# Block-sparse attention and a gated FFN on one core: later attention outputs turned by DMA, a bank of its own for the values, the block mask's spreading matrix made on chip, filler matmuls early, the last FFN groups interleaved

## The chip, the core and the metric

The kernel runs on one core of a Trainium2 chip. Its time is the device time in microseconds (us) of one execution; lower is better. A core has five engines with queues of their own, each of which works its instructions off in order: TensorE (PE in the profile, with PEld for its weight loads), VectorE (DVE), ScalarE (ACT), GpSimd (POOL) and SyncE (SP), which here only issues DMAs. Matmuls write to PSUM, which the kernel divides into eight banks of 2 KB per partition.

## The reference

Attention over 4 batches, 8 heads, 768 tokens and 64 channels, with a mask in blocks of 32 tokens: a block pair is kept when the blocks are neighbours, when one of them is the first or the last, or when it was drawn at random. What attention gives goes, as 3072 rows of 512, through a gated FFN.

```python
scores = scale * np.matmul(q, k.transpose(0, 1, 3, 2))
mask = np.abs(blk_i - blk_j) <= window
mask = mask | (blk_i == 0) | (blk_j == 0) | (blk_i == n_blocks - 1) | (blk_j == n_blocks - 1)
for qb in range(n_blocks):
    for kb in sampled_blocks[qb]:
        mask[qb * block:(qb + 1) * block, kb * block:(kb + 1) * block] = True
scores = np.where(mask, scores, -1000000000.0)
scores = scores - np.max(scores, axis=-1, keepdims=True)
attn = np.exp(scores)
attn = attn / (np.sum(attn, axis=-1, keepdims=True) + 1e-09)
out = np.matmul(attn, v)
x = np.ascontiguousarray(out.transpose(0, 2, 1, 3)).reshape(B * S, H * D)
gate = 1.0 / (1.0 + np.exp(-(x @ w_gate)))
return (gate * (x @ w_val) @ w_out).astype(np.float32)
```

## The kernel before

The work is cut into 12 pieces n (batch b = n // 3, a third c = n % 3 of the queries, 256 of them), and each piece into 4 pairs of heads p. For each pair:

- **scores**: three groups tt of four matmuls (L444) write transposed scores to `st`, a buffer of two banks of which there are two. They use 64 rows of the PE array, two heads side by side ("row" mode).
- **exp** on ACT (L454) from `st` to `pt`, then the multiplication with the 0/1 mask on DVE (L462).
- **values**: 24 matmuls (L476) into `o`, one bank. A column of ones beside the values gives the sums, so that DVE's reciprocal (L484) and multiplication (L487) leave the attention output `x16` with tokens on partitions.
- **turn**: two PE transposes (L500) by the identity turn `x16` into `tT`, which sits in the same bank `o`, and ACT copies it (L505) to `xT`, where channels are on partitions. So each pair goes through the one bank `o` twice.

The **FFN** takes the pieces in the groups [0], [1,2], ... [9,10], [11], that is 256 or 512 tokens at a time. For each of 12 slices f of the hidden width, PE makes gate and value (L525, four matmuls each) in the two banks `gv`; ACT takes the tanh (L540), DVE makes `h` (L545). For each 128 tokens, 12 matmuls (L556) sum the output in `py`, one bank; DVE halves it (L568) into `y`, and SP stores it (L572).

At the **start**, SP loads k, q and v of batch 0 as float32 (L280), 12 transfers of 384 KB. ACT, DVE and POOL cast them to float16 (L305, L295); PE turns k and q by transposes into `gv` (L317), and ACT or DVE copies them out (L321). The mask comes from a 24x24 table of blocks (DVE, L385 to L391), which is spread to tokens with the help of `e24`, a 24x768 matrix of zeros and ones loaded from DRAM by ACT's queue (L261): a product into a buffer `st` (L397, L398), a copy (L401), and then two matmuls for each mask tile (L411) and a copy (L421). The FFN weights follow by POOL's DMA queue (L362, L371). k and q of batches 1 to 3 are cast on POOL and turned by DMA transposes from SP (L329).

**What sets the order.** The kernel records each step as an operation with an engine, a duration, its buffers and a priority; `Plan.run` plays them through on a clock of its own and emits the instructions of each engine in the order that comes out. Smaller priorities go first: attention has 0 to 143, the FFN 10000 and more, so the FFN fills PE where attention isn't ready. Each engine works in order, so an instruction that waits holds up all that stands behind it on that engine.

Of the kernel before, what the change touches and what calls it, by code (L numbers as in the profile page):

```python
# [16 lines left out]
BLK = 32  # L17
# [3 lines left out]
NCH = 3  # L21
# [5 lines left out]
VW = 66  # L27
GROUPS = [[0], [1, 2], [3, 4], [5, 6], [7, 8], [9, 10], [11]]
# [27 lines left out]
class Plan:  # L56
# [3 lines left out]
    def __init__(self):  # L60
        self.ops, self.rings, self.queued = [], {}, {}

# [25 lines left out]
    def run(self):  # L88
# [23 lines left out]
        while left:  # L112
            wake = []
            for e in LAT:
# [4 lines left out]
                for o in todo[e]:  # L119
# [28 lines left out]
                    break  # L148
                if best is None:
                    continue  # L150
# [11 lines left out]
                if o.dma:  # L162
                    dma_free = max(dma_free, now + 1.5) + o.dma
                    o.seen = dma_free + 0.5
                else:
                    o.seen = o.end + o.lat
# [26 lines left out]
def kernel(  # L193
# [14 lines left out]
    tok = NJ * np.arange(128)[None, :] + np.arange(NJ)[:, None]  # L208
    e24_np = (tok.reshape(1, -1) // BLK == np.arange(NB)[:, None]).astype(np.float16)
    e24_h = nc.inline_tensor(e24_np, name="bb_e24")  # L210
# [17 lines left out]
    for name, n in (  # L228
# [3 lines left out]
    ):  # L232
        P.ring(name, n, name != "gv")
# [13 lines left out]
    def one(shape, dt, name):  # L247
# [5 lines left out]
        ident16 = one([128, 128], f16, "ident16")  # L253
# [3 lines left out]
    e24 = one([NB, S], f16, "e24")  # L257
    P.op("ACT", 0.5, lambda: nc.scalar.dma_start(ident16(), id_h.ap()), writes=[ident16], prio=-90, dma=0.3)
    P.op("ACT", 0.5, lambda: nc.scalar.dma_start(sbi(), sampled_blocks), writes=[sbi], prio=-89, dma=0.1)
    P.op("ACT", 0.5, lambda: nc.scalar.dma_start(mi(), mi_h.ap()), writes=[mi], prio=-88, dma=0.1)  # L260
    P.op("ACT", 0.5, lambda: nc.scalar.dma_start(e24(), e24_h.ap()), writes=[e24], prio=-87, dma=0.1)  # L261

    vring = [one([128, 2, NJ, VW], f16, f"v16_{i}") for i in range(8)]
    for i in range(8):
        P.op(
            "POOL", 0.1,
            lambda i=i: nc.gpsimd.memset(vring[i]()[:, :, :, 64:VW], 1.0),
            writes=[vring[i]], prio=-80 + i,
        )

# [4 lines left out]
    def load(nm, b, p, prio, after=(), sync=None):  # L275
# [12 lines left out]
        loads[nm, b, p] = P.op("SP", 0.5, go, writes=[t], prio=prio, after=after, dma=1.22)  # L288

    def cast_v(b, p, prio):  # L290
# [3 lines left out]
            "POOL", 1.0,  # L294
# [4 lines left out]
    def cast_qk(nm, b, p, prio, eng):  # L299
# [3 lines left out]
        P.op(  # L303
            eng, {"ACT": 0.83, "DVE": 0.56, "POOL": 0.95}[eng],
# [4 lines left out]
    def turn_pe(nm, b, p, prio, eng, out_eng):  # L309
        cast_qk(nm, b, p, prio, eng)  # L310
# [8 lines left out]
        P.op("PE", 0.6, go, reads=[c, ident16], writes=[g], prio=prio, mode="full")  # L319
        f = nc.scalar.copy if out_eng == "ACT" else nc.vector.tensor_copy  # L320
        P.op(out_eng, 0.8 if out_eng == "ACT" else 0.55, lambda: f(t(), g()), reads=[g], writes=[t], prio=prio)  # L321

# [14 lines left out]
    for i, (nm, p) in enumerate(order0):  # L337
        if nm == "v":
            last_v = cast_v(0, p, -40 + i)
            if p == 2:  # L340
                gate_w = last_v
        else:
            turn_pe(
                nm, 0, p, -40 + i,
                {"k": "ACT", "q": "DVE"}[nm] if p == 0 else "POOL",
                "ACT" if p == 0 and nm == "k" else "DVE",
# [11 lines left out]
    for a, z in zip(edges, edges[1:]):  # L358
        for nm, t, s in (("g", wg, wgv), ("v", wv, wvv)):
# [4 lines left out]
            o = P.op("POOL", 0.8, go, after=[gate_w], prio=-20 + n, dma=(z - a) * 3.3 / 512)  # L364
# [3 lines left out]
    for s in range(3):  # L368
# [3 lines left out]
            after=[gate_w], prio=-20 + n, dma=3.3,  # L372
# [6 lines left out]
    sbf = one([NB, 3], f32, "sbf")  # L379
    eqs = [one([NB, NB], f32, f"eq{n}") for n in range(3)]  # L380
    mb16, mb24 = one([NB, NB], f16, "mb16"), one([NB, S], f16, "mb24")
    mask = one([128, NCH, NCH, 512], f16, "mask")

    def blocks():
        nc.vector.tensor_copy(sbf(), sbi().bitcast(u16)[:, 0:12:4])  # L385
        for n in range(3):
            nc.vector.tensor_scalar(
                eqs[n](), in0=mi()[:, NB:], scalar1=sbf()[:, n : n + 1], scalar2=None, op0=ALU.is_equal
            )
            nc.vector.tensor_tensor(mi()[:, 0:NB], mi()[:, 0:NB], eqs[n](), op=ALU.max)  # L390
# [236 lines left out]
```

## Time and profile before

| | us |
|---|---|
| median of 8 runs (320.4 to 324.08) | 321.14 |
| the profiled execution, its own time | 320.89 |
| its span (first to last instruction) | 319.1 |
| PE busy, 2852 matmuls | 299.2 |
| DVE busy, 374 instructions | 203.4 |
| ACT busy, 279 instructions | 195.8 |
| POOL busy, 69 instructions | 51.8 |

The span is 1.8 us shorter than the execution's own time. Busy time of PE is modelled with the ends of pipelined matmuls, so a busy PE isn't one at its peak. The rows that follow in the prediction are of this one execution: the chain of work that ended last (start, length, what), windows (busy time in a stretch, number of instructions, granted clock, DMA share, GB/s), groups of instructions (count, busy us, mean ns, idle before and what ended it) and the timeline (start, length, engine, line, operation, xcount, idle before it).

### The profile page before, as it was taken

What the parts mean: (1) busy time and instruction counts of PE and PEld (TensorE: products, weight loads), DVE (VectorE), ACT (ScalarE), POOL (GpSimd) and SP (SyncE); (2) the same over time, 40 slices, a digit from 0 to 9 for tenths busy, and PEclk for the clock granted to TensorE, in tenths of its full rate; (3) what the DMA queues carried; (4) which work ended last, traced back from release to release, by engine and by line L of the source; (5) the groups of instructions that cost most, each with busy time, mean ns of one, the idle gap of its engine ahead of it and who ended that gap; (6) DMA issues with size and microseconds to landing.
All of it is one profiled execution on the core that took longest, in us unless ns stands there. A gap on an engine that the chain in (4) does not pass through costs nothing.

```text
span 319.1 us, 6860 instructions
## 1 busy us (share of the span) xinstructions
PE 299.2 (94%) x2852; PEld 160.7 (50%) x2852; DVE 203.4 (64%) x374; ACT 195.8 (61%) x279; POOL 51.8 (16%) x69
## 2 busy tenths in 40 slices
PE   1998889999999999999999999999999999999994
PEld 1464556644455454545455553455554454445661
DVE  2789988457787877767786687466776343333331
ACT  3569996566788856787995788565686321221120
POOL 1892016453451441000000000000000000000000
PEclk9999999999999999999999999999999999999999
DMA  7999999999995674000001100001000010001101
GB/s 232 335 136 205 205 299 294 295 280 272 326 286 184 92 182 125 33 2 3 0 35 42 59 2 1 2 33 68 35 2 0 1 68 33 35 0 66 69 0 66
DMA packets 41804, 35.12 MB, mean 110 GB/s; under 512 B 20757, under 2 KB 38701, under 8 KB 41773
## 3 DMA queue, kind: packets, MB, share of 16 engines
q1 hardware_dynamic: 35712, 29.89, 33.2%
q0 software_dynamic: 5808, 4.72, 9.6%
q8 instruction: 22, 0.36, 0.5%
q10 hardware_dynamic: 252, 0.08, 0.1%
q14 instruction: 10, 0.07, 0.1%
HBM read 28.39 MB, written 6.29 MB: 109 GB/s over the span
## 4 chain that ended last, share of the span: by engine, by line
PE 68%; ACT 6%; DVE 4%; issue 1%; DVEq 0%; ACTq 0%
PE gv L525 32%; PE py L556 19%; PE o L476 8%; PE st L444 7%; ACT pt L454 5%; PE o L500 1%; DVE h L545 1%; DVE pt L462 1%; ACT tg L540 1%; DVE y L568 1%; DVE x L487 0%; ACT x L505 0%; DVE rz L484 0%; DVEq L545 0%; ACTq L540 0%
## 5 line engine op out<-in xcount | busy, mean ns | idle before, releaser
L454 ACT ACTIVATE pt<-st 128x1024 f16<-128x1024 f32 x144 | 142.9, 1042 | 42.8 <-PE st L444 42.2
L462 DVE TENSOR_TENSOR pt<-pt,mask 128x1024 f16<-128x1024 f16 x144 | 104.9, 738 | 33.6 <-ACT pt L454 33.1
L540 ACT ACTIVATE tg<-gv 128x512 f32<-128x512 f32 (+1 forms) x84 | 46.2, 550 | 59.6 <-PE gv L525 56.0
L525 PE MATMUL gv<-x,wv 128*128 128x512 f16 (+1 forms) x336 | 76.1, 349 | 2.2 <-DVE h L545 1.3
L525 PE MATMUL gv<-x,wg 128*128 128x512 f16 (+1 forms) x336 | 76.2, 349 | 0.8 <-ACT tg L540 0.6
L545 DVE SCALAR_TENSOR_TENSOR h<-tg,gv 128x512 f16<-128x512 f32 (+1 forms) x84 | 51.0, 608 | 38.2 <-PE gv L525 35.6
L556 PE MATMUL py<-wo,h 128*128 128x512 f16 x288 | 70.4, 379 | 0.8 <-DVE y L568 0.8
L444 PE MATMUL st<-qT,kT 64*128 64x256 f16 x576 | 51.3, 281 | 4.7 <-ACT pt L454 4.0
L476 PEld LDWEIGHTS <-pt 128*128 128x128 f16 x1152 | 41.7, 98 | 10.6 <-issue 4.6
L525 PEld LDWEIGHTS <-wv 128*128 128x128 f16 x336 | 30.3, 97 | 32.4 <-issue 10.4
L476 PE MATMUL o<-v,pt 128*128 128x65 f16 x1152 | 45.2, 194 | 0.0
L525 PEld LDWEIGHTS <-wg 128*128 128x128 f16 x336 | 30.3, 98 | 27.0 <-issue 5.2
L556 PEld LDWEIGHTS <-h 128*128 128x128 f16 x288 | 26.1, 98 | 28.4 <-issue 3.4
L444 PEld LDWEIGHTS <-kT 64*128 64x128 f16 x576 | 21.7, 95 | 33.3 <-issue 29.3
L568 DVE TENSOR_SCALAR y<-py 128x512 f32<-128x512 f32 x24 | 16.5, 690 | 19.9 <-PE py L556 19.9
L505 ACT COPY x<-o 128x256 f16<-128x256 f16 x48 | 18.7, 390 | 8.5 <-PE o L500 8.5
L487 DVE TENSOR_TENSOR x<-o,rz 128x256 f16<-128x256 f32 x48 | 20.4, 425 | 1.7
L305 POOL CAST k<-ks 128x768 f16<-128x768 f32 x15 | 14.2, 947 | 43.5 <-DMA ks<-in_k_dram 26.0
L295 POOL CAST v<-vs 128x768 f16<-128x768 f32 x16 | 15.3, 953 | 17.3 <-DMA vs<-in_v_dram 10.1
L305 POOL CAST q<-qs 128x768 f16<-128x768 f32 x15 | 14.0, 936 | 11.3 <-DMA qT<-q 7.7
L484 DVE RECIPROCAL rz<-o 128x4 f32<-128x4 f32 x48 | 8.6, 179 | 11.0 <-PE o L476 10.6
L500 PE MATMUL o<-ident,x 128*128 128x128 f16 x96 | 13.5, 222 | 0.5 <-DVE x L487 0.5
(31 smaller groups left out, 51.1 us busy)
## 6 DMA issues: line engine op xcount, KB each, us to landing
ks<-in_k_dram SPq DMA_DIRECT2D x16, 384.0 KB, 6.2
qs<-in_q_dram SPq DMA_DIRECT2D x16, 384.0 KB, 6.0
vs<-in_v_dram SPq DMA_DIRECT2D x16, 384.0 KB, 5.2
out_dram<-y SPq DMA_DIRECT2D x24, 256.0 KB, 2.0
wo<-in_moe_w_out_dram POOLq DMA_DIRECT2D x3, 512.0 KB, 19.0
wg<-in_moe_w_gate_dram POOLq DMA_DIRECT2D x2, 512.0 KB, 9.7
wv<-in_moe_w_val_dram POOLq DMA_DIRECT2D x2, 512.0 KB, 12.0
wg<-in_moe_w_gate_dram POOLq DMA_DIRECT2D x2, 256.0 KB, 5.4
```

The costliest lines, as they stand in the source:

```text
L305: lambda: f(c(), s().rearrange("p h j d -> p j h d")),
L444: nc.tensor.matmul(st()[:, hd, jj * CH : (jj + 1) * CH], kT[r, 2 * tt + jj, :], qT[r, 2 * c : 2 * c + 2, :], start=True, stop=True,)
L454: lambda st=st, pt=pt: nc.scalar.activation(pt().rearrange("p h j q -> p h (j q)"), st(), AF.Exp, scale=SCALE),
L462: nc.vector.tensor_tensor(t, t, mask()[:, c, tt].unsqueeze(1).to_broadcast([128, 2, 512]), op=ALU.mult)
L476: nc.tensor.matmul(o()[:, 2 * jq + hd, 0:65], pts[j // 2]()[:, hd, j % 2, jq * 128 : jq * 128 + 128], v_[:, hd, j, 0:65], start=(j == 0), ...
L487: lambda: nc.vector.tensor_tensor(x16().rearrange("p j (h d) -> p (j h) d", d=64), o()[:, :, 0:64], rz().to_broadcast([128, 4, 64]), op=AL ...
L505: lambda: nc.scalar.copy(dst()[:, i * CH : (i + 1) * CH], tT().rearrange("p j q -> p (j q)")),
L525: nc.tensor.matmul(t()[:, 0:w], wt()[:, i, f * 128 : (f + 1) * 128], xT[g, i]()[:, 0:w], start=(i == 0), stop=(i == NP - 1),)
L540: lambda tg=tg, t=pair[0]: nc.scalar.activation(tg()[:, 0:w], t()[:, 0:w], AF.Tanh, scale=0.5),
L545: lambda tg=tg, t=pair[1], h_=h_: nc.vector.scalar_tensor_tensor(h_()[:, 0:w], tg()[:, 0:w], 1.0, t()[:, 0:w], op0=ALU.add, op1=ALU.mult),
L556: nc.tensor.matmul(py(), hts[g, f]()[:, tt * 128 : (tt + 1) * 128], wo()[:, f], start=(f == 0), stop=(f == NF - 1),)
L568: "DVE", 0.69, lambda py=py, y=y: nc.vector.tensor_scalar_mul(y(), py(), 0.5),
```

## The change

Seven things change.

1. **Turn by DMA.** From piece 3 on (`TURN_PE`), SP turns `x16` into `xT` by a DMA transpose; the two PE transposes and ACT's copy remain for pieces 0 to 2 alone. `x16` has four buffers instead of two.
2. **Own bank for values.** `o` holds values alone; the PE turn of pieces 0 to 2 goes to `py`.
3. **Mask blocks on chip.** `e24` is no longer loaded: POOL makes it by a memset and two AFFINE_SELECT. The block table takes four DVE operations instead of eight, the spreading is done by third (256 columns) instead of at once, and the masks of pieces 1 and 2 come later. The three small loads of ACT's queue change order.
4. **Filler matmuls.** DVE clears a tile `zero`; where the plan has PE idle before its time 26 and `py` is free, it puts in a matmul of zeros into `py`.
5. **Start.** `vs` has three buffers; kT of pair 1 is copied by ACT; the weights' loads start behind the last cast of q instead of that of v's pair 2.
6. **FFN's end.** The last group's slices have priorities between those of the group before, and every other slice uses a buffer `st` for both products; the last two groups' outputs alternate between `o` and `py`; the last 128 tokens are done in two halves of 256 columns. Group 0's outputs wait for all of its `h`, and all outputs wait for all of `wo`.
7. **Planner.** Most of its durations and its DMA time change, which shifts the order everywhere.

```diff
-        ("qs", 3), ("ks", 3), ("vs", 2), ("q16", 2), ("k16", 2), ("qT", 8), ("kT", 8),
-        ("v16", 8), ("pt", 12), ("rz", 2), ("x16", 2), ("tg", 2), ("y", 3),
+        ("qs", 3), ("ks", 3), ("vs", 3), ("q16", 2), ("k16", 2), ("qT", 8), ("kT", 8),
+        ("v16", 8), ("pt", 12), ("rz", 2), ("x16", 4), ("tg", 2), ("y", 3),
...
+                if best is None and e == "PE" and now < self.spin_until and self.spin.writers[0].seen is not None:
+                    s = slot("py")
+                    if s is not None and s <= now and self.spin.writers[0].seen <= now:
+                        best = self.spin_op()
...
-    P.op("ACT", 0.5, lambda: nc.scalar.dma_start(e24(), e24_h.ap()), writes=[e24], prio=-87, dma=0.1)
+    def spread_tokens():
+        nc.gpsimd.memset(e24(), 1.0)
+        for sign, base in ((1, 0), (-1, BLK - 1)):
+            nc.gpsimd.affine_select(
+                e24(), e24(), [[sign, NJ], [sign * NJ, 128]], ALU.is_ge, 0.0,
+                base=base, channel_multiplier=-sign * BLK,
+            )
+    P.op("POOL", 2.0, spread_tokens, writes=[e24], prio=-81)
...
+            "PE", 0.1, lambda: nc.tensor.matmul(t(), zero(), zero(), start=True, stop=True),
...
-                "ACT" if p == 0 and nm == "k" else "DVE",
+                "ACT" if p <= 1 and nm == "k" else "DVE",
...
+        p24 = psb("py" if c == 0 else "gv", [NB, CH])
+                p24(), mb16(), e24()[:, 2 * c : 2 * c + 2].rearrange("b j q -> b (j q)"), start=True, stop=True
...
-        tT, dst = psb("o", [128, 2, 128], f16), xT[g, p]
+        dst = xT[g, p]
+        if n >= TURN_PE:
+            P.op(
+                "SP", 0.55,
+                lambda: nc.sync.dma_start_transpose(
+                    dst()[:, i * CH : (i + 1) * CH].rearrange("p (j q) -> p j q", j=2),
+                    x16().rearrange("p j m -> p (j m)"),
+                ),
+                reads=[x16], writes=[dst], prio=seq - 5, dma=0.45,
+            )
+            return
+        tT = psb("py", [128, 2, 128], f16)
...
+        last = g == len(GROUPS) - 1
+        first = seq - 90 if last else seq
+            if last and f % 2:
+                both = psb("st", [128, 2, 512])
+                pair = [(both, 0), (both, 1)]
...
-                    after=[w_in[nm, f]], prio=seq + f, mode="full",
+                    after=[w_in[nm, f]], prio=first + f * 0.5, mode="full",
...
+            parts = 2 if last and tt == w // 128 - 1 else 1
+                py = psb("o" if g >= len(GROUPS) - 2 and (tt + u) % 2 else "py", [128, DM])
...
-                    "PE", 0.862, go, reads=[hts[g, f] for f in range(f0, f0 + 4)], writes=[py],
-                    after=[w_out[f] for f in range(f0, f0 + 4)], prio=seq + 12 + tt, mode="full",
+                        "PE", 0.862 / parts, go, reads=[hts[g, f] for f in range(NF if g == 0 else f0 + 4)], writes=[py],
+                        after=list(w_out.values()), prio=seq + 12 + tt, mode="full",
```

Where the order moves, three places are shown; lines left out repeat.

**PE at the start, before** (k and q with their numbers are pairs 0 and 1 in turn, `mb` the block table, `e` is `e24`):

```order
L317 MATMUL gv<-ident_66,k_116 128x128
...
L317 MATMUL gv<-ident_66,q_127 128x128
...
L317 MATMUL gv<-ident_66,k_148 128x128
...
L397 MATMUL st<-e_69,mb_85 24x512
...
L317 MATMUL gv<-ident_66,q_159 128x128
...
L444 MATMUL st<-qT,kT 128x256
```

The same place after the change (`zero` is the filler, `k_129` and `q_147` are pair 0, `k_170` is pair 1):

```order
L289 MATMUL py<-zero 128x128
...
L424 MATMUL py<-e_69,mb_83 24x256
...
L341 MATMUL gv<-ident_66,k_129 128x128
...
L341 MATMUL gv<-ident_66,q_147 128x128
...
L436 MATMUL gv<-mb_0_84,e_69 128x256
...
L467 MATMUL st<-qT,kT 128x256
...
L341 MATMUL gv<-ident_66,k_170 128x128
```

Eight fillers and the product with `e24` now stand ahead of the first transposes, and the first two groups of scores ahead of pair 1's transposes instead of behind them. On POOL, where before the `v` memsets came first, the start reads after the change (an ISA row has no tile of its own):

```order
L270 MEMSET e_69 24x768
L272 ISA
L272 AFFINE_SELECT e_69<-e_69 24x768 x2
L282 MEMSET v_0_71 128x12x2
...
L329 CAST k_170<-ks 128x768
L329 CAST q_181<-qs 128x768
```

Three rows more stand ahead of everything that POOL did. **SP about pieces 2 and 3, before**, the transposes of batch 1's last k and q between the loads of batch 2:

```order
L329 DMA_TRANSPOSE kT<-k_1216 128x6x128
L280 DMA ks<-in_k_dram 128x2x384
L329 DMA_TRANSPOSE qT<-q_1240 128x6x128
L280 DMA qs<-in_q_dram 128x2x384
L280 DMA vs<-in_v_dram 128x2x384
L572 DMA out_dram<-y 128x512
```

and after it:

```order
L354 DMA_TRANSPOSE kT<-k_1242 128x6x128
L304 DMA ks<-in_k_dram 128x2x384
L354 DMA_TRANSPOSE qT<-q_1297 128x6x128
L304 DMA qs<-in_q_dram 128x2x384
L523 DMA_TRANSPOSE x_1336<-x_1299 128x2x128
L304 DMA vs<-in_v_dram 128x2x384 x2
L354 DMA_TRANSPOSE kT<-k_1363 128x6x128
L304 DMA ks<-in_k_dram 128x2x384
L619 DMA out_dram<-y 128x512
```

The transposes of `x16` (36 in all, the first shown) stand between loads and transposes that wait for POOL. **PE at the end, before** (the last group's last slice, then its outputs, of which the first waits for the last `h` and the second for the bank):

```order
L525 MATMUL gv<-x_4361,wv 128x256
...
L556 MATMUL py<-wo,h_4713 128x512
...
L556 MATMUL py<-wo,h_4547 128x512
...
L556 MATMUL py<-wo,h_4754 128x512
```

and after it:

```order
L603 MATMUL o<-wo,h_4496 128x512
...
L563 MATMUL gv<-x_4202,wg 128x256
...
L563 MATMUL st<-x_4202,wg 128x256
...
L603 MATMUL py<-wo,h_4518 128x512
...
L603 MATMUL o<-wo,h_4518 128x256
...
L603 MATMUL py<-wo,h_4518 128x256
```

Two slices of the last group now follow a whole output of the group before (the `h` with 44 in front), in turn in `gv` and `st`, and the three last outputs lie in three turns of two banks. In all, PE has 96 - 24 = 72 transposes fewer and 23 fillers more, and its changes between row mode and full mode go from 188 to 194.

More of the change, by code (lines that the diff above doesn't have):

```diff
@@ L393 @@
-    P.op("DVE", 1.8, blocks, reads=[sbi, mi], writes=[sbf, mb16, *eqs], prio=-70)
-    p24 = psb("st", [128, 1024])
-    def spread_blocks():
-        nc.tensor.matmul(p24()[0:NB, 0:512], mb16(), e24()[:, 0:512], start=True, stop=True)
-        nc.tensor.matmul(p24()[0:NB, 512:768], mb16(), e24()[:, 512:768], start=True, stop=True)
-    P.op("PE", 0.8, spread_blocks, reads=[mb16, e24], writes=[p24], prio=-70, mode="full")
-    P.op("DVE", 0.95, lambda: nc.vector.tensor_copy(mb24(), p24()[0:NB, 0:768]), reads=[p24], writes=[mb24], prio=-70)
@@ new lines, with build_mask @@
+    P.op("DVE", 0.65, blocks, reads=[sbi, mi], writes=[mb16, eqs], prio=-70)
+    mask_ops = {}
+    def build_mask(c, prio, after=()):
+        p24 = psb("py" if c == 0 else "gv", [NB, CH])
+        P.op(
+            "PE", 0.2,
+            lambda: nc.tensor.matmul(
+                p24(), mb16(), e24()[:, 2 * c : 2 * c + 2].rearrange("b j q -> b (j q)"), start=True, stop=True
+            ),
+            reads=[mb16, e24], writes=[p24], after=after, prio=prio, mode="full",
+        )
+        f = nc.scalar.copy if c == 0 else nc.vector.tensor_copy
+        P.op("ACT" if c == 0 else "DVE", 0.4, lambda: f(mb24[c](), p24()), reads=[p24], writes=[mb24[c]], prio=prio)
@@ L464, in masks @@
                 )
[L466 removed]
+            P.op("DVE", 0.61, masks, reads=[pt], writes=[pt], after=[mask_ops[c, tt]], prio=seq)
             pts.append(pt)
```

164 lines of the change are left out of this document (88 added, 76 removed).

## The prediction

> **What bounds the kernel now.** I read the page's totals and its chain of work first, then windows along the run.
>
> ```profile
> span 319.1 us, 6860 instructions
> PE 299.2 (94%) x2852; PEld 160.7 (50%) x2852; DVE 203.4 (64%) x374; ACT 195.8 (61%) x279; POOL 51.8 (16%) x69
> ...
> PE 68%; ACT 6%; DVE 4%; issue 1%; DVEq 0%; ACTq 0%
> ...
> core 0: us, PE busy (x), PEclk, DMA share, GB/s
> 4.80:22.60 17.80, 15.32 (x122) 1.00 0.92 251
> 22.60:36.00 13.40, 11.00 (x170) 1.00 1.28 204
> 36.00:64.00 28.00, 25.55 (x351) 1.00 1.18 283
> 64.00:100.00 36.00, 35.05 (x366) 1.00 1.12 298
> 100.00:260.00 160.00, 158.84 (x1545) 1.00 0.14 37
> 288.00:319.10 31.10, 25.46 (x158) 1.00 0.13 51
> ```
>
> PE is busy for 94% of the span and carries 68% of the chain, no other engine over 6%. The windows say where that holds: from 64 to 260 PE idles 0.95 + 1.16 = 2.1 us in 196, so a matmul that goes there shortens the run by its own time, and work taken from ACT or DVE alone is worth nothing. PE idles at the two ends: 4.8 + 2.5 + 2.4 us up to 36, and 5.6 us in the last 31. So the change has three terms: the turns between 64 and 264, the end, and the start.
>
> **The turns.** The chain's rows give PE's advance, free of the modelled overlap.
>
> ```profile
> 259.12 1.73 PE py L556 x8
> 260.84 0.11 PE o L500 x2
> 260.96 1.73 PE gv L525 x8
> ...
> L500 PE MATMUL o<-ident,x 128*128 128x128 f16 x96 | 13.5, 222 | 0.5 <-DVE x L487 0.5
> ```
>
> The group's 222 ns of one transpose overlap with their neighbours; in the chain a pair of them costs 0.11 us between two blocks of matmuls. Pieces 3 to 11 have 36 pairs of heads: 36 x 0.11 = **4.0 us saved**. ACT's 36 copies go with them, worth nothing here since PE is the bound. In their place stand 36 DMA transposes on SP. They can stay hidden: in pieces 3 to 10 the FFN group that needs an `xT` comes behind another group that is still unfinished, and for piece 11 group 5's products are left as cover. If that cover were gone, PE would wait for an issue and a landing each time (rows below). The changes of mode go from 188 to 194, three returns more at about the same 0.11 each: **+0.3**.
>
> The bank of its own for `o` lets the values of the next pair start without the turn and its copy. From 64 on that is worth little: the windows have no idle PE for it to remove. I put it at zero there and count it at the start.
>
> **The end.** The chain again:
>
> ```profile
> 289.04 0.87 PE gv L525 x8
> 289.91 2.66 PE py L556 x12
> ...
> 300.74 1.03 PE gv L525 x8
> ...
> 303.65 0.61 PE gv L525 x4
> ...
> 304.83 0.61 PE gv L525 x4
> ...
> 310.70 0.99 PE py L556 x4
> 311.71 0.70 DVE y L568
> 312.45 2.76 PE py L556 x12
> 315.24 0.69 DVE y L568
> ...
> L545 DVE SCALAR_TENSOR_TENSOR h<-tg,gv 128x256 f16<-128x256 f32 x24 | 10.0, 416 | 9.3 <-PE gv L525 9.3
> ```
>
> At 289 eight narrow FFN matmuls take 0.87 (0.109 each) and twelve output matmuls 2.66 (0.22 each). From 300.74 on a slice of eight takes 1.18 (303.65 to 304.83), since the two banks `gv` come free only behind tanh and `h`, and nothing else is left for PE. Between 300.74 and 312.45 the order has 60 narrow matmuls and 12 output ones: 60 x 0.109 + 12 x 0.216 = 9.1 of 11.7 us, so 2.6 us are waiting, 0.7 of it for DVE to empty `py`. With every other slice in `st`, two output banks, and group 5's outputs spread between the slices, I see no wait left but some 0.2 at new handovers: -2.4. A little before 300.74 the same wait stands once more (0.3). The last halving is done on 256 columns; a DVE operation on 256 columns takes 416 ns where the wide one takes 690, so -0.3. Together **-3.0**, between -1.5 (if `h` of the last slices comes late) and -3.4.
>
> **The start.** The timeline, ACT's group for 4 to 22.6, and two DMA rows:
>
> ```profile
> 0.73 0.46 POOL L267 MEMSET v<- 128x24 f16 x8 [0.29 <-POOLq L611]
> 2.65 1.28 ACT L305 ACT_TABLE_LOAD   x1 [2.65 <-issue]
> 4.83 0.82 PE L317 MATMUL gv<-ident,k 128*128 128x128 f16 x6 [4.83 <-ACT k L305]
> 7.63 0.82 POOL L305 CAST k<-ks 128x768 f16<-128x768 f32 x1 [6.44 <-DMA ks<-in_k_dram]
> 11.41 4.25 ACT L454 ACTIVATE pt<-st 128x1024 f16<-128x1024 f32 x4 [4.92 <-PE st L444]
> 21.45 1.02 ACT L454 ACTIVATE pt<-st 128x1024 f16<-128x1024 f32 x1 [1.60 <-PE st L444]
> 22.62 3.79 ACT L454 ACTIVATE pt<-st 128x1024 f16<-128x1024 f32 x4
> 35.45 0.60 PE L525 MATMUL gv<-x,wg 128*128 128x256 f16 x4
> ...
> L454 ACT ACTIVATE pt<-st 128x1024 f16<-128x1024 f32 x8 | 8.1, 1022 | 7.9 <-PE st L444 7.8
> L321 ACT COPY kT<-gv 128x768 f16<-128x768 f16 x1 | 0.8, 798 | 0.9 <-PE gv L317 0.9
> ...
> qs<-in_q_dram SPq DMA_DIRECT2D x16, 384.0 KB, 6.0
> wv<-in_moe_w_val_dram POOLq DMA_DIRECT2D x2, 512.0 KB, 12.0
> ```
>
> Here ACT sets the pace once it has work: from 22.6 on an exp follows the other every (3.79 - 1.02) / 3 = 0.92 us. Before, eight exps take until 22.47 because ACT waits 7.8 us for scores, which stand on PE behind pair 1's transposes and the mask's products.
>
> After the change PE's ninth matmul is the product with `e24`, and everything of PE stands behind it. `e24` is ready when POOL has done a memset of 768 elements, the ISA row, and two AFFINE_SELECT. For memset and selects the nearest row is POOL's cast of 768 elements, 0.82 (at least 0.06, the pitch of the small memsets; at most twice the cast). **The ISA row is the unknown**: no row of before has it. It stands ahead of the first AFFINE_SELECT alone, so I take it for something that this operation needs loaded. The ends are 0.1 (a small row of POOL) and 12.0 (the slowest DMA of the start, issued by POOL). A table load of ACT takes 1.28, but a load from DRAM in this stretch, with the DMA engines 0.92 busy, takes 6.0 from issue to landing; I take 6.0, since new code would come that way. Then `e24` is ready at 0.73 + 0.82 + 6.0 + 1.64 = 9.2. From there two sets of transposes (0.82 each), a copy (0.8) and three short products with their handovers (0.45 each, an estimate) lead to the first exp at 9.2 + 3.8 = 13.0 instead of 11.41. But then scores no longer wait for pair 1: eight exps at 0.92, with kT's copy (0.8) now between them, end at 13.0 + 7.4 + 0.8 = 21.2, against 22.47: **-1.3**. POOL's casts start 2 us later, at 9.7, and each still precedes its transposes.
>
> The Trainium skill (GPSIMD Engine Reference, section 2.1, Instruction dispatch) says that the first call to a freshly loaded kernel of GpSimd pays a load of about 6 us with no instruction of its own in the profile. By it the sum would be the same within 0.1; by ACT's 1.28 it would be 4.7 lower. No run so far shows it.
>
> Further, the FFN's first matmul comes behind 18 groups of scores instead of 22, four exps or 3.7 us earlier; PE idled 13.4 - 11.0 = 2.4 us in 22.6 to 36, of which 3.7 / 13.4 is **-0.7** (between 0 and -2.4). The four shorter table operations of DVE, the other order of the small loads, `vs` with three buffers and the weights' gate lie beside the wait for `e24`: nothing.
>
> The fillers, lastly:
>
> ```profile
> 21.77 0.40 PE L500 MATMUL o<-ident,x 128*128 128x128 f16 x2
> 25.00 0.29 PE L500 MATMUL o<-ident,x 128*128 128x128 f16 x2
> ```
>
> The same pair takes 0.40 before 22 and 0.29 after, though the granted clock is 1.00 in every window: PE starts slow. It stayed slow through 8.5 to 22 with hardly a gap. Eight fillers ahead of a stop of 6 us won't change that, so I count them as nothing. The Trainium skill (TensorE: Matmul & The Clock Gate, Part 1) has the clock rise after about 3.4 us of sustained work; by that rule fillers right up to the first transposes would save some 0.3 on each of three steps, a sum lower by about 0.9. The trace, with 13 us of nearly full slow work, speaks against a saving that early.
>
> **Sum.** -4.0 + 0.3 - 3.0 - 1.3 - 0.7 = -8.7: span 310.4. The profiled execution took 1.8 more than its span, so **312.2 us**, 2.8% under the median of 321.14; the profiled execution (320.89) lies 0.25 under that median, which I leave in the range.
>
> **Rivals.**
>
> - *The load is cheap* (1.28 or less): `e24` is no later than the block table, the first exp comes near 8, and up to 4.7 more is saved: 307.5. For it: the one load of an engine's tables that the trace has, ACT's, takes no longer. Chance 0.15.
> - *The load is dear* (12.0): 6 more at the start, 318.2. For it: the DMA engines are full then. Chance 0.15.
> - *Freed PE time comes back as waits*: the order is tighter now, an instruction of PE that stands right where its input was planned waits for ACT or DVE, and the 4.0 and 0.7 are lost: 316.9. Against it: FFN matmuls stand between most steps. Chance 0.14.
> - *SP blocks, slower than before*:
>
> ```profile
> 49.62 3.03 SPq L329 DMA_TRANSPOSE qT<-q  x1
> ...
> kT<-k SPq DMA_TRANSPOSE x12, 4.8
> ```
>
> A transpose holds SP for up to 3.03 us while loads run, and lands 4.8 after its issue. Eight turns of pieces 3 and 4 stand in that stretch between loads and transposes that wait for POOL. `x16` has four buffers: once a turn takes longer than four pairs of heads take (some 18 us, as 36 pairs fill about 200 us at 5 each), DVE's next `x16` stops, and with it masks and `h`, the FFN, and PE. Eight stops of a whole cycle, 3.03 + 4.8 less the 5 of a pair, are 8 x 2.8 = 23 us, half of it hidden by the FFN's matmuls in stock: 312.2 + 11 = 323. Against it: a turn would have to wait through several loads. Chance 0.06.
>
> The forecast (309.5 to 315.5) has 0.50. The range, 306.5 to 318.7, takes in both ends of the load. A measurement of this kernel can tell about 0.5% (1.6 us) from no change: faster than 319.5 has 0.50 + 0.15 + 0.13 + 0.11 = 0.89 less 0.03 for what I don't see, 0.86; within 0.5% 0.07; slower 0.07.
>
> **What would show it.** Right: a gap on POOL of about 6 us before AFFINE_SELECT and PE idle from some 2 to 9 us; the first exp near 13 and the eighth ending near 21; no L500-like pair in the chain after 64; the last 15 us of the chain PE alone, with the last `y` half as long. Wrong: POOL without a gap (first rival); DVE or PE waiting for DMA `x` in 64 to 130 (last rival); "PE o <- DVE pt" or "PE st <- ACT pt" waits of some us in all after 64 (third). The forecast falls if the load is much dearer than a DMA, or if PE's time from 64 to 288 shrinks by less than 3.

## The result and the profile after

| | before | after |
|---|---|---|
| median of all runs, us | 321.34 (32 runs) | 313.53 (11 runs, 311.17 to 317.83) |
| ratio to before | | 0.9743, 95% interval 0.9714 to 0.9771 |
| the profiled execution: time, span | 320.89, 319.1 | 314.06, 312.4 |
| its mean granted clock | 1.00 | 0.978 |

The change makes the kernel 2.6% faster. The forecast was 312.2, with a range of 306.5 to 318.7. Ratios, mean spans and the medians of the experiments leave out runs more than 1.5% above the fastest of their kernel, among them one of 1011.31 us of the kernel with dummies at all turns, whose cause is not known. First come the totals of the page after the change and the shares of its chain of work.

```profile
span 312.4 us, 6854 instructions
PE 297.2 (95%) x2816; PEld 158.8 (51%) x2816; DVE 200.9 (64%) x372; ACT 187.8 (60%) x245; POOL 51.7 (17%) x72
...
PE 87%; DVE 6%; ACT 3%; DMA 2%; issue 1%; ACTq 0%; DVEq 0%
```

PE now carries 87% of the chain instead of 68%. The windows say where PE still idles (columns as before: length, busy time of PE, PEld, DVE, ACT, POOL, granted clock, DMA share, GB/s).

```profile
4.80:22.60 17.80, 13.89 (x159) 8.78 (x161) 12.50 (x22) 10.91 (x13) 13.28 (x17) 1.00 0.88 249
22.60:36.00 13.40, 12.47 (x127) 7.24 (x123) 10.82 (x23) 9.49 (x12) 3.50 (x5) 0.54 1.27 201
36.00:64.00 28.00, 24.99 (x348) 16.50 (x346) 23.47 (x47) 23.62 (x37) 11.35 (x12) 0.98 1.16 287
64.00:100.00 36.00, 34.84 (x344) 17.88 (x340) 26.63 (x46) 25.18 (x33) 12.49 (x16) 1.00 1.09 271
100.00:260.00 160.00, 160.00 (x1560) 79.93 (x1557) 108.85 (x203) 106.06 (x128) 8.02 (x9) 1.00 0.23 58
288.00:312.40 24.40, 20.85 (x147) 14.07 (x144) 9.63 (x20) 4.46 (x12) 0.00 (x0) 1.00 0.17 65
```

From 100 to 260 PE doesn't idle at all, and at the end the 5.6 us of idle have become 3.6, of which 3.1 lie behind PE's last matmul (the last `y`, its store and the end of the program). New is the second row: a granted clock of 0.54, where before it was 1.00 throughout. The timeline of the start shows what came in the place of the wait that was forecast.

```profile
0.80 0.73 POOL L270 MEMSET e<- 24x768 f16 x1 [0.29 <-POOLq L658]
1.61 1.77 POOL L272 TENSOR_SCALAR_AFFINE_SELECT e<-e 24x768 f16<-24x768 f16 x2
...
1.82 0.43 ACTq L267 DMA_DIRECT2D ident<-bb_ident  x1
...
7.09 0.80 PE L341 MATMUL gv<-ident,k 128*128 128x128 f16 x6 [1.63 <-DMA ident<-bb_ident]
...
10.82 1.02 ACT L477 ACTIVATE pt<-st 128x1024 f16<-128x1024 f32 x1 [2.10 <-PE st L467]
...
16.35 4.17 DVE L485 TENSOR_TENSOR pt<-pt,mask 128x1024 f16<-128x1024 f16 x4
...
21.13 0.29 PE L534 MATMUL py<-ident,x 128*128 128x128 f16 x2 [1.19 <-DVE x L510]
...
35.36 1.04 PE L563 MATMUL gv<-x,wg 128*128 128x256 f16 x4
```

The selects begin 0.08 us after the memset (1.61 against 0.80 + 0.73): the ISA row costs nothing that can be seen. But the identity, whose load is now the third on ACT's queue, is needed at 5.5 and there only at 7.05. At 21.13 PE waits 1.19 for `x16`, since DVE's four multiplications ahead of it took 1.04 each. Finer windows of the same profile show the clock.

```profile
16.00:24.00 8.00, 5.40 (x91) 3.56 (x87) 7.93 (x14) 6.10 (x8) 7.90 (x12) 0.98 0.80 103
24.00:36.00 12.00, 11.80 (x120) 6.97 (x118) 9.45 (x20) 8.24 (x11) 2.10 (x3) 0.50 1.26 204
36.00:38.00 2.00, 2.00 (x16) 0.77 (x14) 1.51 (x3) 0.87 (x2) 0.00 (x0) 0.67 1.24 203
38.00:40.00 2.00, 2.00 (x35) 1.34 (x34) 1.70 (x4) 1.95 (x4) 0.00 (x0) 1.00 1.24 206
```

PE is busy for only 5.40 of 8 us in 16 to 24; from 23.8 to some 37.5 it gets half its clock. The last part of the chain, up to the last `y`, is PE alone:

```profile
295.38 2.59 PE py L603 x12
297.97 0.87 PE gv L563 x8
298.84 0.87 PE st L563 x8
299.72 2.59 PE o L603 x12
302.31 0.87 PE gv L563 x8
303.18 0.88 PE st L563 x8
304.05 2.59 PE py L603 x12
306.64 1.31 PE o L603 x12
307.95 1.32 PE py L603 x12
```

A slice of eight matmuls takes 0.87 as in the full flow, not 1.18; no wait for `h` or for the bank is left.

**The clock sorts the runs, roughly.** Every run lists its span and mean granted clock. The five runs of the changed kernel at 0.994 or more have a mean span of 310.3, the four at 0.978 one of 312.8; but one at 0.995 took 311.8 and one at 0.989 only 310.1. Of 49 runs of the kernel before that were taken beside the experiments, 39 have 0.993 or more, most of them 1.00, with a mean of 318.9. At a good clock the change is thus worth 8.6 us, and it gets a good clock more seldom. In what follows a span "at a good clock" is the mean of a kernel's runs at 0.993 or more (two to six of them), and a look is a profiled run.

Two limits hold for small differences of such spans. The experiments ran on three chips, and the kernel before itself takes 318.7 at a good clock on the chip of most of them, 319.4 on that of the runs with dummies at all turns and with another number in the planner, and 318.9 on that of the runs with dummies at two turns. And runs of one kernel at a good clock differ by 2 us. So less than about 1 us between two kernels says little, and the ratio, taken against the kernel before on the same chip, is the safer figure.

### The profile page after: what moved, and what is told of

Read it like the earlier page. It is cut to its first block, busy times and chain, and to the rows that moved or that the text cites. A ratio compares the mean times of both kernels' runs of the same rounds, so it can differ in the third digit from the quotient of the medians.

```text
span 312.4 us, 6854 instructions
## 1 busy us (share of the span) xinstructions
PE 297.2 (95%) x2816; PEld 158.8 (51%) x2816; DVE 200.9 (64%) x372; ACT 187.8 (60%) x245; POOL 51.7 (17%) x72
## 4 chain that ended last, share of the span: by engine, by line
PE 87%; DVE 6%; ACT 3%; DMA 2%; issue 1%; ACTq 0%; DVEq 0%
PE gv L563 38%; PE py L603 18%; PE st L467 12%; PE o L499 12%; DVE pt L485 4%; ACT pt L477 2%; PE o L603 2%; PE st L563 2%; DMA ident<-bb_ident 2%; PE gv L436 1%; PE gv L341 1%; DVE x L510 1%; PE py L534 1%; PE py L289 0%; ACT tg L578 0%
## 5 line engine op out<-in xcount | busy, mean ns | idle before, releaser
L578 ACT ACTIVATE tg<-gv 128x512 f32<-128x512 f32 (+1 forms) x78 | 43.0, 551 | 64.8 <-PE gv L563 57.4
L563 PE MATMUL gv<-x,wg 128*128 128x512 f16 (+1 forms) x312 | 72.9, 356 | 1.3 <-ACT tg L578 1.2
L563 PE MATMUL gv<-x,wv 128*128 128x512 f16 (+1 forms) x312 | 72.7, 355 | 0.7 <-DVE h L585 0.4
L585 DVE SCALAR_TENSOR_TENSOR h<-tg,gv 128x512 f16<-128x512 f32 (+1 forms) x78 | 48.6, 623 | 34.5 <-PE gv L563 21.3
L603 PE MATMUL py<-wo,h 128*128 128x512 f16 (+1 forms) x264 | 61.5, 375 | 0.0
L499 PE MATMUL o<-v,pt 128*128 128x65 f16 x1152 | 46.8, 197 | 0.9 <-DVE pt L485 0.9
L603 PEld LDWEIGHTS <-h 128*128 128x128 f16 x300 | 27.9, 98 | 30.7 <-issue 3.0
L467 PEld LDWEIGHTS <-kT 64*128 64x128 f16 x576 | 21.2, 96 | 33.9 <-issue 30.0
L614 DVE TENSOR_SCALAR y<-py 128x512 f32<-128x512 f32 (+1 forms) x22 | 14.9, 679 | 19.0 <-PE py L603 19.0
L289 PE MATMUL py<-zero 128*128 128x128 f16 x23 | 6.1, 265 | 1.6 <-DVE zero L264 1.1
L603 PE MATMUL o<-wo,h 128*128 128x512 f16 (+1 forms) x36 | 7.3, 344 | 0.0
```

Of the source, the lines that this page charges most:

```text
L467: nc.tensor.matmul(st()[:, hd, jj * CH : (jj + 1) * CH], kT[r, 2 * tt + jj, :], qT[r, 2 * c : 2 * c + 2, :], start=True, stop=True,)
L499: nc.tensor.matmul(o()[:, 2 * jq + hd, 0:65], pts[j // 2]()[:, hd, j % 2, jq * 128 : jq * 128 + 128], v_[:, hd, j, 0:65], start=(j == 0), ...
L563: nc.tensor.matmul(t()[:, z, 0:w], wt()[:, i, f * 128 : (f + 1) * 128], xT[g, i]()[:, 0:w], start=(i == 0), stop=(i == NP - 1),)
L578: lambda tg=tg, a=pair[0]: nc.scalar.activation(tg()[:, 0:w], a[0]()[:, a[1], 0:w], AF.Tanh, scale=0.5),
L585: lambda tg=tg, a=pair[1], h_=h_: nc.vector.scalar_tensor_tensor(h_()[:, 0:w], tg()[:, 0:w], 1.0, a[0]()[:, a[1], 0:w], op0=ALU.add, op1=A ...
L603: nc.tensor.matmul(py()[:, m], hts[g, f]()[:, tt * 128 : (tt + 1) * 128], wo()[:, f, m], start=(f == 0), stop=(f == NF - 1),)
```

## The experiments

The theory is that the turns and the end are worth what the prediction gave them, and the start is not. There are two rivals: the freed time overlaps, so that undoing one part costs little; or the start's gain is there, but covered by the late identity or eaten by the clock.

**Turns back on PE.**

```diff
-TURN_PE = 3
+TURN_PE = 12
-        tT = psb("py", [128, 2, 128], f16)
+        tT = psb("py" if n < 3 else "o", [128, 2, 128], f16)
```

> The changed kernel with the attention outputs of all pieces turned by PE again (in bank o from piece 3 on, as before), so 72 transposes on PE and 36 copies on ACT more, 36 DMA transposes fewer; the planner's order follows. Theory A (PE is the bound between 64 and 288, so each pair of transposes counts 0.11): 4.0 us more, 317 to 318. Rival B (the turns lay beside other work, or DMA turns cost as much by waits): within 1 us of 313.5. Rival C (handing the bank o over twice per pair costs more than the transposes themselves): 320 or more.

The median is 319.04 us, the ratio 0.9922 (0.9886 to 0.9957); the span at a good clock is 316.1, 5.7 more than that of the changed kernel. Rival B is out, and the size lies between A and C. Rows of its chain show what a pair of transposes costs PE:

```profile
150.30 0.11 PE o L534 x2
...
165.11 0.22 PE o L534 x2
...
167.82 0.54 PE st L467 x8
168.36 0.97 PE py L603 x4
169.33 0.11 PE o L534 x2
```

A pair between other matmuls in full mode advances PE by 0.11, as forecast. The one at 165.11 follows scores (row mode) directly and advances it by 0.22; but four output matmuls directly behind scores take 0.97 as well, where they take 0.86 elsewhere, so these 0.11 are the return from row mode and not the turn's own. What the turns cost on top is a wait: PE idles 1.0 us more between 64 and 260 than in the changed kernel. The rest of the 5.7 isn't located; the two means are known only to about 1 us.

**The turns by DMA alone**, in the kernel before (the same DMA call for n >= 3, and `("x16", 4)`).

> The kernel before with one thing of the change: from piece 3 on the attention outputs are turned by DMA transposes on SP, with four buffers x16; the turns of pieces 0 to 2 stay in the bank o. Theory A (each pair of transposes is worth 0.11, as the chain of before showed): 4.0 less than the kernel before, 317. Theory A2 (the run with all turns on PE was 5.7 above the changed kernel, so a turn costs more than its own 0.11: the bank o is handed over twice and what stands behind waits): 5.5 to 6 less, 315 to 315.5. Rival B (the DMA turns cost something of their own, which the changed kernel hides only with its own order): 318 to 321.

The median is 316.72 us, the ratio 0.9868 (0.9832 to 0.9903), that is 4.2 us, close to A's 4.0. The span at a good clock, 314.1, is 4.8 less than before; but the runs of this kernel take 2.1 us beside their span, where the others take 1.7 to 1.8, so the span flatters it and the ratio counts. No cost of SP shows. So the turns are worth 4 alone, and up to 6 where their undoing brings new waits.

**The old end in the changed kernel.**

```diff
-        last = g == len(GROUPS) - 1
+        last = False
-                py = psb("o" if g >= len(GROUPS) - 2 and (tt + u) % 2 else "py", [128, DM])
+                py = psb("py", [128, DM])
```

> The changed kernel without the interleaved end: the last group's slices behind the group before, all in the two gv banks, and every output through py. Theory A (the end is worth the 2.6 us of waits and the half y that the chain of before showed): 316 to 317, with the waits of some 0.5 us per slice back in the last 20 us. Rival B (the planner fills the end elsewhere): within 1 us of 313.5. Since the clock's stretch at 0.50 varies from run to run by up to 3 us, compare profiles of equal clock.

The median is 316.28 us, the ratio 0.9861 (0.9818 to 0.9903); the span at a good clock is 314.7, 4.4 more than that of the changed kernel. Theory A holds, and the chain has the waits of before again:

```profile
301.82 0.43 DVE h L585
...
302.30 0.61 PE gv L563 x4
...
309.19 0.70 DVE y L614
...
309.93 2.77 PE py L603 x12
```

**Turns and end together, with the start of before** (the kernel of the experiment with the turns by DMA alone, with the FFN function of the changed kernel and `py` freed in any order).

> The kernel before with the turns by DMA from piece 3 on and with the whole new end of the FFN, but with the start of before: identity loaded first, the spreading matrix loaded, no fillers, the old planner durations. Theory A (with all turns on PE the changed kernel lost 5.7, with the old end 4.0, and the whole change is worth only 7.8, so its start brings nothing or costs up to 2): 310.5 to 313, no slower than the changed kernel's 313.5, and a granted clock of 0.998 or more in most runs, as in the kernel before. Rival B (the start is worth the 2.0 that the prediction gave it): 315 to 316. Rival C (the sizes overlap, since what one edit frees another fills): 313 to 314.5 with a clock like that of the changed kernel.

The median is 313.3 us, the ratio 0.976 (0.9726 to 0.9795); all six runs have a clock of 0.993 or more, and the mean span is 311.5. So the end is worth 314.1 - 311.5 = 2.6 here by the spans, and 316.3 - 313.3 = 3.0 by the times of the same runs. What remains to the changed kernel, 311.5 - 310.3 = 1.2 at a good clock, is the new start together with the values' own bank and the planner's new durations; it is at the edge of what these runs can tell, and nothing in the median. The time lies in Rival C's band, 0.3 above Theory A's, and the clock is that of Theory A; Rival B is out.

**No fillers** (`lambda: None` instead of the matmul of zeros; the 23 rows are left out).

> The changed kernel without its 23 filler matmuls; the order is otherwise the same. Changed kernel: 313.5 us, ratio 0.974; PE's matmuls become fast at 13.5 us, and the granted clock then falls to 0.50 from 23.8 to 37.5. Theory A (fillers bring nothing in the sum: PE warms earlier, and the stretch at half clock takes the gain back): 311 to 315 us, with PE slow up to about 20 us or later, no stretch at 0.50, and a mean clock of 0.995 or more. Rival B (fillers pay): 316 or more, the first exps late. Rival C (without the early warming the half-clock stretch goes and nothing is lost): 309 to 311. If the stretch at 0.50 is there without fillers too, the fillers don't cause it.

The median is 313.1 us, the ratio 0.9762 (0.9731 to 0.9793): no difference that can be measured. PE stays slow until about 23, much as in the kernel before, where with fillers it was fast from 13.5 on. In 24 to 36 the clock is 1.00; the look has one stretch at half clock, 3.4 us long, at 57. So Theory A holds for the time and for the slow PE, but not for the clock: three of the six runs have 0.982 or 0.984, where it forecast 0.995 or more.

**Identity first** of ACT's three small loads (the two others behind it).

> The changed kernel with the identity's load first of ACT's three small loads, as in the kernel before, and the order of all else the same. Theory A (the identity, landing at 7.05 us, holds the first transposes and with them the start): it lands near 2 us, the first transposes run near 5 us, the first exp near 9 instead of 10.8, and the time is 1.5 to 2 us shorter, 311.5 to 312. Rival B (the casts on POOL and the copies behind them set the pace of the next pairs anyway): first exp earlier but the eighth exp's end unchanged near 20.2, time within 0.5 us of 313.5. Rival C (the block table now lands late instead, and the mask's product, which stands ahead of the first transposes in PE's order, holds them as long): no gain, PE waiting for the copy of the mask's blocks.

The median, 311.92 us, lies in Theory A's band, but the ratio, 0.9751 (0.9711 to 0.9792), and the span at a good clock, 310.4, are those of the changed kernel. Rival C came true: the block table was late instead (its product ran at 6.92 instead of 5.08), so that the transposes ran at 7.24 instead of 7.09 and the first exp at 11.00.

**Identity made on chip**, its load left out:

```diff
-lambda: nc.scalar.dma_start(ident16(), id_h.ap())
+lambda: None
+        nc.gpsimd.memset(ident16(), 1.0)
+        for sign in (1, -1):
+            nc.gpsimd.affine_select(
+                ident16(), ident16(), [[sign, 128]], ALU.is_ge, 0.0, base=0, channel_multiplier=-sign,
+            )
```

> The changed kernel with the identity made on POOL, behind the spreading matrix, by a memset and two AFFINE_SELECT, and its load left out; the order of all else is the same. Theory A (the identity's load, landing at 6.5 to 8.3 us in the looks so far, sets the start): first transposes near 5.4, first exp near 9.2 instead of 10.8, and the time 1 to 2 us less, 311.5 to 312.5 and 309 to 310 at a clock of 0.994 or more. Rival B (POOL's casts of pairs 1 to 3 and DVE's multiplications set the pace behind the first two exps): first exp near 9.2, but the ninth exp and the FFN's first matmul unchanged, time within 0.5 of 313.5. Rival C (the casts on POOL are pushed back by the three instructions): later than 313.5.

```profile
5.43 0.82 PE L345 MATMUL gv<-ident,k 128*128 128x128 f16 x6
...
20.67 0.29 PE L538 MATMUL py<-ident,x 128*128 128x128 f16 x2 [1.48 <-DVE x L514]
```

The timeline has the first transposes at 5.43 and the first exp at 9.19, 1.6 earlier; but PE's first turn comes only 0.5 earlier, at 20.67 instead of 21.13, behind a longer wait for DVE. The ratio is 0.9748 (0.9695 to 0.9802), as that of the changed kernel. Two runs at a good clock have spans of 310.0 each; three of the six had clocks of 0.962 to 0.973 and took 316.4 to 317.7 us, among them the look, with half clock from 22.7 to 46.7. These 310.0 are just Theory A's 310, but the changed kernel has 310.3 itself, so of the 1.6 no more than 0.3 is seen, less than these few runs can tell. That is Rival B's case, though the ninth exp does come 0.7 earlier: from 16 to 24 DVE is busy for 7.93 of 8 us, here as in the changed kernel, and what comes earlier waits for DVE.

**All turns by DMA** (`TURN_PE = 0`).

> The changed kernel with the outputs of pieces 0 to 2 turned by DMA as well, so that no PE turn stands in PE's order behind DVE's x16; the planner's order follows. Theory A (the trace of the changed kernel has three waits of PE for x16 in 16 to 64 us, 3.2 us in all, ahead of turns of pieces 0 to 2; without the turns PE goes on to the next scores): 1.5 to 3 us less, 310.5 to 312, and fewer stretches at half clock, since PE idles less before 24 us. Rival B (ACT or DVE have no room, so the scores behind wait instead for the exps): within 0.7 of 313.5. Rival C (with the DMA engines more than fully shared between 20 and 40 us the turns land late, and the FFN's first group comes late): 314.5 or more.

The median is 330.47 us, the ratio 1.0303 (1.0265 to 1.0341), slower than the kernel before: Rival C, and far more than it expected. SP's timeline shows why, and so does the answer for the tile `x`:

```profile
21.37 18.18 SPq L523 DMA_TRANSPOSE x<-x  x6
42.65 0.37 SPq L304 DMA_DIRECT2D ks<-in_k_dram  x1
```

```profile
DMA to landing us min/median/max: 3.6/7.1/11.8
```

Between 20 and 40, with the DMA engines' share at 1.0 to 1.9, six turns hold SP for 18.2 us; those of 20 to 75 land after 7.1 (median) where the changed kernel's take 2.3; batch 1's loads go out behind them, and the FFN's first matmul moves to 50.4. From 36 to 100 PE idles for 16.7 of 64 us, where it idles for 4.2 in the changed kernel. It also gets half its clock in two stretches, of 13.7 and 24 us, so that a part of the 17 us lost against the changed kernel (330.5 - 313.5) is the clock's; how large a part was not separated.

**PE kept busy at the turns.** Dummy transposes of zeros ahead of each PE turn:

```diff
         def turn():
+            for _ in range(8 if n == 0 and p < 2 else 4):
+                for jq in range(2):
+                    nc.tensor.transpose(tT()[:, jq, :], zero(), ident16())
             for jq in range(2):
```

> The changed kernel with dummy transposes of zeros (into the same bank, overwritten) ahead of each PE turn of pieces 0 to 2: 16 for the first two turns, 8 for the other ten, about 0.06 us each at full clock, at the places where the trace has PE waiting for x16. The order is otherwise the same. Theory A (the stretch at half clock comes from PE idling 2.6 of 8 us in 16 to 24; if PE is kept busy there, the clock stays): mean clock 0.994 or more in all runs, 311 to 312, against 0.978 and 314 to 315 in four of the eleven undisturbed runs of the changed kernel. Rival B (the clock's stretches come by themselves, whatever PE does): the same mix of clocks as the changed kernel, time 313.5 or up to 2 more, since dummies stand in PE's way. Rival C (dummies delay the scores): 315 or more at a good clock.

```profile
16.00:24.00 8.00, 6.35 (x109) 4.62 (x107) 7.93 (x13) 5.38 (x7) 7.69 (x11) 1.00 0.62 77
24.00:36.00 12.00, 11.61 (x196) 8.15 (x193) 11.70 (x25) 10.96 (x16) 3.28 (x5) 1.00 1.27 199
```

The windows that had 0.98 and 0.50 have 1.00, and all runs have a clock of 0.995 or 1.00: Theory A is right on the clock. But the time is 314.07 us, the ratio 0.9771 (0.9727 to 0.9816), no better than the changed kernel's. The span is 312.3, which is 7.1 less than that of the kernel before on this chip, against 8.6 for the changed kernel. The 112 dummies at 0.06 are 6.7 us of PE, and only part of that can lie in waits.

**Dummies at the first two turns alone** (6 and 0 in the place of 8 and 4), **and the same with the identity on chip.**

> The changed kernel with 12 dummy transposes of zeros ahead of each of the first two PE turns alone, where PE waited 1.2 and 0.7 us for x16; 112 dummies at all twelve turns kept the clock at 0.995 or more but cost about what they saved. Theory A (the long stretch at half clock that begins near 24 us comes from PE's waits in 16 to 24, and 24 dummies that lie within these waits cost nothing): no stretch at half clock before 30, mean clock 0.989 or more, span 309.5 to 311 in most runs, median 311.5 to 312.5. Rival B (later waits, at 28 to 36 and 55 to 60, bring the stretch as well): clocks of 0.978 as often as in the changed kernel, median 313.5. Rival C (the dummies delay the turn): 314 or more at a good clock.

> The same with the identity made on chip as well, so that the first exp comes near 9.2. Theory A (DVE is busy without a gap from 14 to 24 and sets the pace of the first pieces, so an earlier first exp is worth nothing, as the run with the identity on chip alone showed at equal clocks): the time of the run with dummies alone, within 0.7 us. Rival B (there the earlier start was only hidden by its stretch at half clock of 24 us): 1 to 1.5 us less than the run with dummies alone, 310 to 311.

The medians are 314.16 us, ratio 0.9775 (0.9735 to 0.9816), and 314.39 us, ratio 0.9784 (0.9739 to 0.9829). The long stretch at 24 is gone in both looks, and no run is below 0.982; but shorter stretches remain (near 55 and 65 in the look without the identity; a mean of 0.989 in nine of the twelve runs), and the time isn't better than the changed kernel's. With the dummies alone the clock followed Theory A, while the time is the 314 or more of Rival C, though only one of these runs had a good clock. With the identity as well Theory A holds: its earlier start brings nothing here either. The look of this last kernel took 317.77 us, 2 to 4 more than its other runs, and its waits have a row that no other look has:

```profile
PE gv L570 <- DMA x<-x: 3.3, 2, 1.8
```

One turned output, of a piece behind the first three, lands 6.9 us after 106 there, and PE waits for it.

**Another number in the planner**: 1.0 instead of 0.61 for the first six multiplications of DVE.

> The changed kernel with one number of the planner changed: the first six mask multiplications of DVE are planned with 1.0 us, near what the trace shows there (four take 4.17), instead of 0.61. The order follows: pair 0's values go behind the transposes of pair 3's k, and PE's first turn behind two more groups of scores. Theory A (the planner's order put PE behind DVE's x16, 1.2 us at the first turn, and the wait costs its own time): 1 us less, 312 to 312.7, and PE's wait for x16 under 2 us instead of 3.2. Rival B (DVE is busy without a gap from 14 to 24 us and sets the pace; another order of PE can't help): within 0.5 of 313.5 at an equal clock.

The median is 316.09 us, the ratio 0.9843 (0.9797 to 0.9889), slower than the changed kernel. PE's wait for `x16` fell to 0.6 as hoped, but waits for `gv` of 2.9 us (tanh 1.7, `h` 1.2) came up in 14 to 64. Neither theory gave this. No kernel tried here beats the changed one by more than can be measured.

## Why the prediction came out as it did

- **The bound** was read rightly: PE's own time counts from 64 on. After the change 160.00 of 160 us are busy from 100 on. The rival that freed time comes back as waits is out: PE's waits from 64 to 260 are 1.2 us, against 1.9 before.
- **The turns** were put at 4.0. Alone they gave 4.2 by the ratio, and undone they cost 5.7, of which 1.0 is new idle time of PE. The mechanism and the 0.11 a pair hold. The +0.3 for three more returns from row mode was not measured by itself; the 0.11 each that it took is what the chain above shows.
- **The end**, -3.0, lies between the runs' 2.6 (3.0 in time) and 4.4. The waits and the half `y` went as the chain of before had it.
- **The start** is where a step failed: "I take 6.0, since new code would come that way". The ISA row cost under 0.1, and no row here shows the 6.0. The rival of the cheap load (307.5) didn't come in its place either, since PE waited for the identity until 7.05, a load that the prediction had put aside ("the other order of the small loads ... nothing"). So the first exp came at 10.82, between the forecast's 13.0 and the rival's 8, and the eighth exp ended near 20.2 against a forecast of 21.2. That the late identity cost no time that can be measured is shown by the two runs with an early one. What holds the time instead seems to be DVE's pace, a term that the sum lacked: DVE is busy for 7.93 of 8 us from 16 to 24 in the changed kernel and in both of these looks. This is read from the traces; no run shortens DVE's work.
- **The FFN 3.7 earlier**: at half clock it began at 35.36, as before. Where the clock stayed, it began at 33.0 (no fillers) and 32.2 (identity first), some 3 us earlier. That belongs to the 1.2, so of the -1.3 and the -0.7 together some 1.2 was found (1.3 in time), and by another way than they were worked out.
- **The fillers** were right at nothing in the time, for a wrong reason. They did warm PE earlier (at 13.5 in the changed kernel, where the kernel before had 22, and before 17 in eight of ten looks with them), which the prediction had ruled out; the time did not follow.
- **The clock** was missing from the prediction. The times at a good clock go from 320.7 by 316.3 (turns) and 313.3 (end) to 312.0, 8.6 in all, against a forecast of 8.7 and 312.2. That the sum fits so well is luck in part: the turns gave 0.7 more than the 3.7 left to them and the changes of mode, and the start and the FFN 0.7 less than 2.0. The medians give 7.8. The mean span of all runs that count is 311.4, 1.1 above that at a good clock; for the kernel before it is 319.3, 0.4 above. So 0.7 of the change goes with the clock; that the clock itself costs it is not shown, since the kernels that keep the clock are no faster. That the long stretch follows from PE's idling in 16 to 24 is borne out by the runs with dummies. It isn't certain in each run: with under 6 of 8 us busy there, three of five looks had it by 24 us; with over 6, none of nine had one before 27 (in six of these PE was still slow for part of that time, and so busier).
- **SP blocks** was a sound rival at the wrong place. From piece 3 on, the turns land after 2.3 (median; 5.4 at most) and PE doesn't wait for them in the changed kernel. At pieces 0 to 2 the same mechanism costs 17 us, the half clock that came with it included. `TURN_PE = 3` lies on the right side of it, but not far: the late turn in the look with dummies and identity on chip cost PE 3.3 us of waiting.

It stays open why DVE's multiplications take 1.04 between 16 and 20, where the kernel before has 0.74 to 0.92 (POOL is busy beside them in both), and how much the stretch of half clock costs by itself: four runs with it had 2.5 us more than five without, yet the kernels that avoid it are no faster by their ratios.

## What to carry to other kernels

A matmul that can be given to a DMA queue with room was worth its own time here, where PE had no gap (4 us for 36 pairs); the same move into a stretch where the DMA engines were full cost four times as much. An earlier first result brought nothing that could be measured where another engine had no gap behind it: look for that engine before a start-up wait is priced. Compare runs at an equal granted clock, and against the kernel before on the same chip, before small parts are weighed.

## What the hardware showed

- An ISA row ahead of POOL's first AFFINE_SELECT cost under 0.1 us. The Trainium skill (GPSIMD Engine Reference, section 2.1, Instruction dispatch) has a load of about 6 us on the first call to a fresh kernel; this trace doesn't show one.
- Half clock came in steps of about 3.4 us: 3.4 in most stretches, 13.7 in the changed kernel, 24 in the one with the identity on chip (there with PE 19.8 of 20 us busy in 24 to 44 at half clock), and both 13.7 and 24 in the one with all turns by DMA. Between 8 us and the stretches that began by 24, the longest wait of PE was 1.19 us in the changed kernel, 1.48 and 1.94 in the other two. The Trainium skill (TensorE: Matmul & The Clock Gate, A second HAM failure mode: psum-queue depth-cycling) says that short idle times between groups of matmuls can make the clock oscillate, which these looks agree with. The Trainium skill (the same page, Part 1) has the clock fall after an idle window of about 3.4 us, which does not fit these waits.
- PE's first rise is not a fixed time after the first matmul: with fillers, of which the first ran at 1.06, it came between 13 and 16 us in eight looks of ten, near 19.4 in the one with another number in the planner, and near 22.5 in the look at the old end, where PE had been busy for 14.01 of the 14.2 us since 8.3.
- A load of 32 KB issued at 0.73 us landed in 1.9; issued at 1.82, behind the first large loads, it took 5.2 (4.6 to 6.4 in other looks).
